# Two and two shift transfers of 128 target rows, and plain fp32 sums for the first two half steps

## The chip, the cores and the metric

The kernel runs on one core of a Trainium2 chip. The metric is the device time of one execution in microseconds. Before the change three runs took 1301.92, 1305.81 and 1307.23 us; their median is 1305.81.

## The reference

```python
def _attn_ref(u, v, z):              # batch 8, S = 2496, D = 256, d_qk = 64
    scores = (1.0 / S) * np.matmul(z, z.transpose(0, 2, 1))
    attn = np.maximum(scores, 0.0) ** 2
    return u * np.matmul(attn, v)

def _moe_ref(x, phi, w1, w2):        # x: 19968 x 256, phi: 256 x 32, 8 experts, 4 slots each
    logits = x @ phi
    d = softmax over the tokens of logits
    slot_input = d.T @ x
    slot_out = relu(slot_input[e] @ w1[e]) @ w2[e]     for every expert e
    c = softmax over the slots of logits
    return c @ slot_out
```

All inputs and outputs are fp32. `x` is the attention output with batch and sequence taken together.

## The kernel before, in words

**Attention.** A batch is cut into five chunks of up to 512 queries, and a chunk into ten *half steps* of 256 keys each (class `Half`, 400 in all). For a half step PE computes the scores of 256 keys against 512 queries, ACT applies relu and square (`r`), the result is split into a high and a low fp16 part (`ph`, `pl`; a cast on ACT or DVE, then a subtraction on DVE), and PE adds three products to the accumulator `acc`: high by v high, high by v low, low by v high (`sums_halves`, `sums_whole`). v is split in the same way by `load_v`'s `high` (ACT) and `low` (DVE), after a scaling by `v_by` that comes from the energy of all ten loads of v (`squares`, `largest`, `scale_v`). The scores are symmetric, so a block above the diagonal is transposed by DVE into `y`, stored to DRAM (`turned`) and fetched later in place of new scores. Scores of half step h+2 are issued between the two phases of the sums of half step h. `finish_chunk` (line 593) multiplies `acc` by `out_by` and by u into `xg`.

**Opening** (lines 964 to 1009). SP issues five loads of z and ten of v. `measure_z` bounds z (DVE), sums the bounds on PE into the PSUM tile `idle`, and makes power-of-two factors. `keep_busy` issues matmuls of ones whose result nothing reads. `prepare_first` (line 411) makes the scores and parts of half steps 0 and 1; ACT measures nine loads of v and DVE one. `scale_v` turns the largest energy around on PE. Then v is split load by load (`split_first_v`) and the loop at line 1010 begins with the sums of half step 0.

**Soft MoE on the side.** For every 1024 finished tokens `groups(q)` (line 633) returns a list of 15 steps, of which the main loop runs one in nearly each half step (line 1017): logits, exponentials, four transposed blocks and one of the exponentials into the SBUF tile `y` (32 partitions by 4 by 576, four times), then the *shifts* (line 627). A shift copies 32 partitions of `y` to one slot of `xt`, so that tokens lie on partitions. Each shift is four transfers of 32 rows. The shifts stand at steps 7, 9, 11 and 13 (line 785), and the last step hands `slot_sums` (line 715) to the next group's `logits`, where PE reads all of `xt` (the trace names these matmuls `lg<-xt`).

**What sets the order.** All engines run in program order. All transfers are issued by SP, one after the other: an SP entry that waits for its source holds up all behind it. Nearly all instructions are recorded under line 74, the wrapper that keeps the order, so they are told apart by the names of their tiles.

Of the kernel before, what the change touches and what calls it, by code (L numbers as in the profile page):

```python
# [77 lines left out]
def attn_soft_moe_kernel(ctx, tc, uT, v, zz, phi, ww, outT):  # L78
# [21 lines left out]


    cw = cpool.tile([P, NG, P], F32, name="cw")
    zt, vt_, zraw = {}, {}, {}

    nudge = cpool.tile([P, 1], F32, name="nudge")
    ones = nc.const_aps.tensor(1.0, [P, 512], BF16)
# [74 lines left out]
    def load_v(b, i):  # L181
        raw = raws.tile([P, 2, D], F32, tag="raw", name=f"vr_{b}_{i}", bufs=NRAW)
        sp.dma_start(raw, v[b, :, 2 * i : 2 * i + 2, :])
        by = v_by[b % 2][:, i : i + 1]
# [52 lines left out]
    def open_loads():  # L237
        for p in range(NP):
            bound, z_splits[p] = load_z(0, p)
            first_z.append(bound)  # L240
        order = [i for p in range(NP) for i in ((2 * p + 1, 2 * p) if p == NQ - 1 else (2 * p, 2 * p + 1))]
        for i in order:
            squares, *two = load_v(0, i)
            first_v.append(squares)
            v_splits.append(two)


    ident = cpool.tile([P, P], F32, name="ident")
# [52 lines left out]
    class Half:  # L301
        def __init__(self, b, ch, p, w, at, part):
            self.b, self.ch, self.p, self.w, self.at = b, ch, p, w, at
            rank = BLOCKS[b == B - 1].index
            mine, keys = rank(ch[0]), rank(p)

            self.turned = keys < mine
            self.turns = keys > mine

            self.opens, self.lends, self.borrows = part == 0, part == 2, part == 3  # L310

            self.padded = ch[0] == NQ - 1
            self.tiles = [4 * p + 2 * w, 4 * p + 2 * w + 1]
            self.begins, self.ends = at == 0, at == 2 * NP - 1

    halves = []
    for b in range(B):
# [90 lines left out]
            ]  # L408
        return [t[:, j] for t in quarters[i]]

    def prepare_first(k):


        r = wa.tile([P, 2, QC], F32, tag="r", name=f"r_{k}", bufs=4)
        pend[k] = hi, lo = high_low(k)
        ps, _ = scores(k)

        def relu():
            act.activation(r, ps, AF.Relu, scale=2.0**-22)

        def square():
            if k:
                act.activation(r, r, AF.Square)
            else:
                dve.tensor_mul(r, r, r)

        def high():
            dve.tensor_copy(hi, r)

        def low():  # L430
            dve.tensor_sub(lo, r, hi)

        return relu, square, high, low

    def prepare(k):

        x = halves[k]
        n = x.ch[2]
# [2 lines left out]
        if x.turned:  # L441
            whole = arriving.pop(k)
            run(middle)
        else:
# [10 lines left out]
        cast = act.copy if x.turned or (x.turns and x.at % 3) else dve.tensor_copy  # L455
        run(turning)
        pieces = [(whole, slice(0, P), cast)]
        if x.borrows:
# [82 lines left out]
    def sums_halves(k, acc, phase, before):  # L541
# [15 lines left out]
        for i in range(len(todo[0])):  # L557
            for h, rows in enumerate(HALF):
                vp, pp = todo[h][i]
                c = h ^ phase ^ side[0]  # L560
                mm = pe.matmul(
                    totals(acc, c, x), vp[rows, c * P : (c + 1) * P], columns(pp[rows], x),
                    start=(x.begins and phase == 0 and i == 0),
                    stop=(x.ends and phase == 1 and i == len(todo[0]) - 1),
                )
                if before is not None:
                    await_(mm, before)
                    before = None
# [6 lines left out]
    def sums_whole(k, acc):  # L575

        x = halves[k]
        hi, lo = pend[k]
        for t, kt in enumerate(x.tiles):
            assert kt < KT - 1  # L580
            vt = vt_[x.b, kt // 2][:, kt % 2]
            for c in range(2):
                for i, (l, r) in enumerate(((0, hi), (1, hi), (0, lo))):
                    pe.matmul(
                        totals(acc, c, x), vt[:, l, c * P : (c + 1) * P], columns(r[:, t], x),
                        start=(x.begins and t == 0 and i == 0),
                        stop=(x.ends and t == 1 and i == 2),
                    )

# [3 lines left out]
    def finish_chunk(b, ch, acc):  # L593
# [3 lines left out]
        while s < n:  # L597
            q, o = divmod(t0 + s, 1024)
            w = min(n - s, 1024 - o)
            if q not in xg_:  # L600
                xg_[q] = wk.tile([P, 2, 1024], F32, tag="xg", name=f"xg_{q}")
            for c in (slice(0, 1), slice(1, 2)) if t0 + n == N else (slice(0, 2),):
                dve.scalar_tensor_tensor(
                    xg_[q][:, c, o : o + w], acc[:, c, s : s + w], out_by[b % 2][:, j : j + 1],
                    ut[:, c, s : s + w], op0=ALU.mult, op1=ALU.mult,
                )
            if o + w == 1024:
                work.extend(groups(q))
            s += w
# [16 lines left out]

    def shift(src, a):


        for b in range(4):  # L630
            sp.dma_start(xt[32 * b : 32 * b + 32, a], src[32 * a : 32 * a + 32, b])

    def groups(q):

# [153 lines left out]

# [167 lines left out]

    idle = acc_ps.tile([P, 2, QC], F32, tag="acc", name="idle")

    def keep_busy(n):
        for _ in range(n):
            for h, rows in enumerate(HALF):
                pe.matmul(idle[:, h], ones[rows, 0:P], ones[rows], start=True, stop=True)
# [10 lines left out]
    def measure_v(n):  # L975
        for _ in range(n):
            first_v.pop(0)()

    def measure_z(js):
        for p in range(*js.indices(NP)):  # L980
# [12 lines left out]
    for f in first[1:]:  # L993
        f()
    second[0]()
    second[1]()
    raise_z(1)
    keep_busy(8)
    first_v.pop()(dve)
    largest(0)  # L1000
    scale_v(0, idle)
    second[2]()
    split_first_v()
    second[3]()
    split_first_v()
    for p in range(2, NP):
        raise_z(p)
    prepare(2)
    acc = None
    for h, x in enumerate(halves):  # L1010
        if x.begins:
# [8 lines left out]
        ahead = [k for k in range(h + 2 + (h > CATCH), h + 3 + (h >= CATCH)) if k < len(halves) and k >= 3]  # L1020
        split_first_v()
        if not ahead and h < 1:
            run(middle)
            run(turning)
            run(behind)
            sums_halves(h, acc, 1, sums_halves(h, acc, 0, None))
        elif ahead and not halves[ahead[0]].turned:
# [318 lines left out]
```

## Time and profile before

| | |
|---|---|
| runs | 1301.92, 1305.81, 1307.23 us, median 1305.81 |
| profiled execution | 1299.81 us, span 1298.0 us |
| PE busy | 1255.5 us, 97% of the span |
| DVE busy | 1100.1 us, 85% |
| ACT busy | 933.3 us, 72% |
| DMA | 297 MB, 74.7% of the 16 DMA engines' span |

The profile shows one execution. PE means TensorE matmuls, PEld its weight loads, DVE VectorE, ACT ScalarE, SP the engine that issues transfers. In a timeline row the columns are start, duration, engine, line, operation, output and inputs, count, and in brackets the idle time just before with what ended it. PEclk is the share of full clock that TensorE was granted: 1.00 is 2.4 GHz, 0.50 is 1.2 GHz. A profiled duration covers an instruction from start to end, and neighbours in one engine's queue overlap by up to 0.1 us.

### The profile page before, as it was taken

Reading aid. Unit: us, or ns where it says so; the run is one execution under the profiler, and the core shown is the slowest. Engines: PE = TensorE matmul, PEld = TensorE weight load, DVE = VectorE, ACT = ScalarE, POOL = GpSimd, SP = SyncE. Lnnn points to the kernel's source line nnn. Section 1 sums busy time; section 2 is a strip of 40 time slices with the busy share of each in tenths; the row PEclk is TensorE's granted clock in tenths of the full one; section 3 lists DMA queues with packets and bytes.
Section 4 is the critical chain, followed back from the end, with each engine's and each line's share of the span. In section 5 each row is a group of like instructions: output and inputs, shape, how many; then the busy total and the mean of one; then the engine's idle time right before and its main releaser. Section 6 shows DMA issues by size and latency. Waiting matters only on the chain.

```text
span 1298.0 us, 27630 instructions
## 1 busy us (share of the span) xinstructions
PE 1255.5 (97%) x10963; PEld 634.2 (49%) x10963; DVE 1100.1 (85%) x1587; ACT 933.3 (72%) x1217; POOL 3.7 (0%) x22
## 2 busy tenths in 40 slices
PE   8999999999999999999999999999999999899984
PEld 3445454545445444545445444454545454345752
DVE  7888898789998899789998799889998799766663
ACT  7878797687857788586958688587976778564553
POOL 0000000000000000000000000000000000000000
PEclk8999999999999999999999999999999999999985
DMA  4868758793888758785788757887587768979769
GB/s 142 239 181 271 226 135 252 242 277 118 202 288 260 241 132 226 256 260 168 186 257 259 252 141 202 266 260 225 145 250 242 265 164 227 288 221 321 290 250 383
DMA packets 136402, 298.88 MB, mean 230 GB/s; under 512 B 17872, under 2 KB 38864, under 8 KB 124240
## 3 DMA queue, kind: packets, MB, share of 16 engines
q1 hardware_dynamic: 136272, 297.11, 74.7%
q8 instruction: 86, 1.41, 0.4%
q14 instruction: 44, 0.36, 0.1%
HBM read 162.04 MB, written 113.77 MB: 212 GB/s over the span
## 4 chain that ended last, share of the span: by engine, by line
PE 72%; DVE 8%; DMA 7%; ACT 5%; SPq 4%; issue 3%; DVEq 0%; ACTq 0%; POOLq 0%
PE acc L74 57%; PE sc L74 9%; SPq L74 4%; DVE y L74 3%; ACT r L74 3%; DVE pl L74 2%; PE lg L74 2%; DMA xt<-y 2%; DMA r<-turned 2%; PE pf L74 2%; ACT ot L74 1%; DMA rd<-lent 1%; ACT ph L74 1%; DVE v L74 1%; DVE ph L74 1%
## 5 line engine op out<-in xcount | busy, mean ns | idle before, releaser
L74 PE MATMUL acc<-ph,v 64*128 64x512 f16 (+5 forms) x5036 | 941.1, 369 | 2.6 <-DVE v L74 1.8
L74 PEld LDWEIGHTS <-v 64*128 64x128 f16 (+1 forms) x7554 | 491.4, 95 | 505.8 <-issue 38.5
L74 PE MATMUL acc<-pl,v 64*128 64x512 f16 (+5 forms) x2518 | 624.6, 368 | 1.7 <-DVE pl L74 1.4
L74 DVE TENSOR_TENSOR pl<-r,ph 128x1024 f16<-128x1024 f32 (+1 forms) x410 | 467.1, 1146 | 110.9 <-ACT ph L74 99.5
L74 ACT CAST ph<-r 128x1024 f16<-128x1024 f32 (+1 forms) x286 | 288.7, 1017 | 124.1 <-DMA r<-turned 55.9
L74 ACT ACTIVATE r<-sc 128x1024 f32<-128x1024 f32 (+1 forms) x242 | 229.0, 946 | 128.7 <-PE sc L74 122.8
L74 ACT ACTIVATE r<-r 128x1024 f32<-128x1024 f32 (+1 forms) x241 | 237.4, 985 | 6.9
L74 DVE STREAM_TRANSPOSE y<-r 128x1024 f32<-128x1024 f32 x160 | 198.0, 1238 | 0.0
L74 PE MATMUL sc<-z,z 64*128 64x512 f16 x912 | 128.1, 376 | 0.4 <-ACT r L74 0.2
L74 PEld LDWEIGHTS <-z 64*128 64x128 f16 x1380 | 75.5, 94 | 70.6 <-issue 2.7
L74 DVE CAST ph<-r 128x1024 f16<-128x1024 f32 (+1 forms) x124 | 74.2, 598 | 12.2 <-ACT r L74 11.6
L74 ACT ACTIVATE v<-vr,v_by 128x512 f16<-128x512 f32 x80 | 57.1, 717 | 9.5 <-DVE v_by L74 8.7
L74 DVE SCALAR_TENSOR_TENSOR xg<-acc,out_by,ut 128x1024 f32<-128x1024 f32 (+7 forms) x57 | 51.5, 926 | 10.0 <-PE acc L74 5.6
L74 DVE SCALAR_TENSOR_TENSOR v<-vr,v_by,v 128x512 f16<-128x512 f32 x80 | 58.5, 732 | 0.1
L74 ACT ACTIVATE vq<-vr 128x512 bf16<-128x512 f32 x79 | 49.2, 622 | 11.4 <-DMA vr<-in_v 11.2
L74 PE MATMUL sc<-z 64*128 64x512 f16 (+1 forms) x468 | 53.0, 321 | 0.0
L74 DVE STREAM_TRANSPOSE y<-xg 128x512 f32<-128x512 f32 x72 | 49.4, 687 | 0.0
L74 DVE COPY ot<-pf 128x1024 f32<-128x1024 f32 (+1 forms) x20 | 24.0, 1198 | 20.8 <-PE pf L74 20.8
L74 ACT COPY ot<-pf 128x1024 f32<-128x1024 f32 (+1 forms) x20 | 19.8, 991 | 24.7 <-PE pf L74 24.7
L74 PE MATMUL lg<-xt 64*32 64x256 f32 x576 | 23.8, 392 | 9.6 <-DMA xt<-y 4.8
L74 ACT CAST ph<-rd 128x512 f16<-128x512 f32 x36 | 21.8, 606 | 12.1 <-DMA rd<-lent 12.1
L74 DVE TENSOR_TENSOR pl<-rd,ph 128x512 f16<-128x512 f32 x36 | 23.9, 664 | 6.2 <-ACT ph L74 6.2
(187 smaller groups left out, 543.7 us busy)
## 6 DMA issues: line engine op xcount, KB each, us to landing
turned<-y SPq DMA_DIRECT2D x320, 256.0 KB, 5.0
r<-turned SPq DMA_DIRECT2D x76, 1024.0 KB, 6.3
xt<-y SPq DMA_DIRECT2D x288, 72.0 KB, 3.6
vr<-in_v SPq DMA_DIRECT2D x80, 256.0 KB, 5.4
outT<-ot SPq DMA_DIRECT2D x18, 1024.0 KB, 6.8
ut<-in_uT SPq DMA_DIRECT2D x31, 512.0 KB, 6.1
lent<-yd SPq DMA_DIRECT2D x144, 64.0 KB, 3.3
rd<-lent SPq DMA_DIRECT2D x36, 256.0 KB, 4.7
```

Of the source, the lines that this page charges most:

```text
L74: return lambda *a, **k: self.tc.keep_in_program_order(f(*a, **k))
```

## The change

**Shifts.** A shift becomes one transfer of 128 target rows: target row 4k+b takes block b of source partition k (before, target row 32b+k). All columns of a row move together, and PE sums over the rows, so the order of rows does not matter. Two shifts are issued at step 7 and two at step 9; steps 11 and 13 do nothing. The last two groups have no shifts in either kernel.

**Opening.** Half steps 0 and 1 no longer wait for the scaled and split v. Their relu and square stay fp32 (`r0`, `r1`), and `plain_sums` multiplies them with the raw fp32 v, in eight fp32 matmuls of 128 by 128 by 512 into a PSUM accumulator `plain`. In half step 4 ACT copies `plain`, scaled by `ratio`, into `xg`, and `finish_chunk` of the first chunk adds `acc` to it before its final product. DVE measures five loads of v and ACT five. The scores of half step 1 go to the accumulator's bank, those of half step 2 are prepared before the loop, and v loads 0 and 1 are split last. `idle` moves to another bank.

```diff
     def shift(src, a):
-        for b in range(4):
-            sp.dma_start(xt[32 * b : 32 * b + 32, a], src[32 * a : 32 * a + 32, b])
+        sp.dma_start(xt[:, a], src[32 * a : 32 * a + 32])
...
-        shifts = [lambda a=a: shift(y(), a) for a in range(4)]
+        shifts = [lambda a=a: (shift(y(), a), shift(y(), a + 1)) for a in (0, 2)]
...
-            todo = [logits, ex, *blocks, e, shifts[0], c0, shifts[1], c1, shifts[2], c2, shifts[3]]
+            todo = [logits, ex, *blocks, e, shifts[0], c0, shifts[1], c1, rest, c2, rest]
...
+    def plain_sums(k, r, acc, t):
+        for c in range(2):
+            pe.matmul(
+                acc[:, c], vraw[k][:, t, c * P : (c + 1) * P], r[:, t],
+                start=(k == 0 and t == 0), stop=(k == 1 and t == 1),
+            )
...
+                sums = acc[:, c, s : s + w]
+                if t0 == 0:
+                    sums = xg_[q][:, c, o : o + w]
+                    dve.tensor_add(sums, sums, acc[:, c, s : s + w])
...
-    keep_busy(6)
+    keep_busy(8)
...
     raise_z(0)
-    keep_busy(1)
-    first = prepare_first(0)
-    first[0]()
-    second = prepare_first(1)
-    measure_v(2 * NP - 1)
+    keep_busy(3)
+    acc = next_acc()
+    r0, relu = first_scores(0, scale=2.0**-30)
+    relu()
+    act.activation(r0, r0, AF.Square)
+    r1, relu = first_scores(1, acc, scale=2.0**-30)
+    relu()
+    keep_busy(4)
     measure_z(slice(1, NP))
...
     raise_z(1)
-    keep_busy(8)
+    dve.tensor_mul(r1, r1, r1)
+    plain_sums(0, r0, plain, 0)
+    r2, relu = first_scores(2)
+    plain_sums(0, r0, plain, 1)
+    measure_v(4, act)
+    measure_v(4, dve)
+    relu()
+    measure_v(1, act)
     first_v.pop()(dve)
     largest(0)
+    plain_sums(1, r1, plain, 0)
     scale_v(0, idle)
+    plain_sums(1, r1, plain, 1)
+    prepare(2, r2)
...
+    landing[4] = [lambda: act.activation(xg_[0][:, :, 0:QC], plain, AF.Identity, scale=ratio)]
+    halves[2].starts = True
+    prepare(3)
...
+        if h < 2:
+            continue
```

**SP's queue in the second batch**, from the first shift of a group to its last. `xt<-y` are the shifts, `r<-turned` and `rd<-lent` fetches, `vr` and `ut` loads of v and u, `turned<-y` stores. Before:

```order
L74 DMA xt<-y_3190 32x576 x4
L74 DMA vr_7_3407<-in_v 128x512
L74 DMA vr_8_3429<-in_v 128x512
L74 DMA ut_3447<-in_uT 128x2x512
L74 DMA vr_9_3449<-in_v 128x512
L74 DMA xt<-y_3190 32x576 x4
L74 DMA rd_3492<-lent_3_3356 128x512
L74 DMA r_3494<-turned_0_4_2496 128x2048
L74 DMA xt<-y_3190 32x576 x4
L74 DMA r_3586<-turned_1_4_2772 128x2048
L74 DMA turned_3_4_3636<-y_3524 32x4x512 x4
L74 DMA xt<-y_3190 32x576 x4
```

With the change:

```order
L74 DMA xt<-y_3119 128x1x576 x2
L74 DMA vr_7_3334<-in_v 128x512
L74 DMA vr_8_3356<-in_v 128x512
L74 DMA ut_3374<-in_uT 128x2x512
L74 DMA vr_9_3376<-in_v 128x512
L74 DMA xt<-y_3119 128x1x576 x2
L74 DMA rd_3417<-lent_3_3285 128x512
L74 DMA r_3419<-turned_0_4_2429 128x2048
L74 DMA r_3507<-turned_1_4_2701 128x2048
L74 DMA turned_3_4_3557<-y_3449 32x4x512 x4
```

The second half of the set now goes out ahead of two fetches and a store that it used to follow, and the set is 4 entries instead of 16.

**PE's queue in the opening**, around the matmul that serves `scale_v` (`idle<-ident,few`). Before:

```order
L74 MATMUL idle_117<-const-bfloat16-1.0 128x512
L74 MATMUL idle_117<-ident_94,few0_92 128x128
L74 MATMUL sc_2_288<-cw_78 128x512 x2
L74 LDWEIGHTS v_0_0_123
L74 MATMUL acc_0_298<-ph_0_202,v_0_0_123 128x512
```

With the change (`plain` is the new accumulator, `vr` raw v):

```order
L74 MATMUL idle_117<-tops0_80,const-float32-1.0 128x4 x2
L74 MATMUL plain_118<-r_0_211,vr_0_0_140 128x512 x2
L74 MATMUL sc_2_247<-cw_78 128x512 x2
L74 MATMUL plain_118<-r_0_211,vr_0_0_140 128x512 x2
L74 MATMUL plain_118<-r_1_217,vr_0_1_142 128x512 x2
L74 MATMUL idle_117<-ident_94,few0_92 128x128
L74 MATMUL plain_118<-r_1_217,vr_0_1_142 128x512 x2
L74 MATMUL sc_3_302<-cw_78 128x512 x2
L74 LDWEIGHTS v_0_2_126
L74 MATMUL acc_0_210<-ph_2_287,v_0_2_126 128x512
```

Plain sums stand where fillers stood, and the first split sums are those of half step 2, behind the scores of half step 3.

**DVE's queue at the end of the first chunk**, from the difference of half step 9 to that of half step 12 (the number behind `pl_` and `ph_` is the half step). Before:

```order
L74 TENSOR_TENSOR pl_9_615<-r_9_608,ph_9_614 128x1024
L74 STREAM_TRANSPOSE y_8_558<-r_9_608 128x2x16x32
L74 CAST ph_10_648<-r_10_642 128x1024
L74 TENSOR_TENSOR pl_10_649<-r_10_642,ph_10_648 128x1024
L74 TENSOR_TENSOR z_0_1_120<-cw_78,z_0_1_120 128x512
L74 CAST ph_11_689<-r_11_683 128x1024
L74 TENSOR_TENSOR pl_11_690<-r_11_683,ph_11_689 128x1024
L74 SCALAR_TENSOR_TENSOR xg_0_705<-acc_0_298,out_by0_90,ut_0_364 128x2x512
L74 TENSOR_TENSOR pl_12_709<-r_12_487,ph_12_708 128x1024
```

With the change:

```order
L74 TENSOR_TENSOR pl_9_564<-r_9_557,ph_9_563 128x1024
L74 SCALAR_TENSOR_TENSOR v_0_0_124<-vr_0_0_140,v_by0_88,v_0_0_124 128x2x256
L74 STREAM_TRANSPOSE y_8_507<-r_9_557 128x2x16x32
L74 CAST ph_10_599<-r_10_593 128x1024
L74 TENSOR_TENSOR pl_10_600<-r_10_593,ph_10_599 128x1024
L74 TENSOR_TENSOR z_0_1_121<-cw_78,z_0_1_121 128x512
L74 SCALAR_TENSOR_TENSOR v_0_1_125<-vr_0_1_142,v_by0_88,v_0_1_125 128x2x256
L74 CAST ph_11_642<-r_11_636 128x1024
L74 TENSOR_TENSOR pl_11_643<-r_11_636,ph_11_642 128x1024
L74 TENSOR_TENSOR xg_0_300<-xg_0_300,acc_0_210 128x2x512
L74 SCALAR_TENSOR_TENSOR xg_0_300<-xg_0_300,out_by0_90,ut_0_312 128x2x512
L74 TENSOR_TENSOR pl_12_662<-r_12_436,ph_12_661 128x1024
```

Two low parts of v and one addition have come in between.

## Rows read from the trace of the kernel before

**Rows 1.** Page, part 1: busy time, share of the span, instructions.
```profile
PE 1255.5 (97%) x10963; PEld 634.2 (49%) x10963; DVE 1100.1 (85%) x1587; ACT 933.3 (72%) x1217; POOL 3.7 (0%) x22
```
**Rows 2.** Windows, PE alone: stretch, length, PE busy, granted clock, DMA share, GB/s.
```profile
25.02:1195.00 1169.98, 1156.08 (x9851) 1.00 0.75 224
```
**Rows 3.** Waits of PE, whole span: total, times, longest.
```profile
PE lg L74 <- DMA xt<-y: 4.8, 7, 1.2
PE lg L74 <- DMA w_raw<-in_w: 4.8, 1, 4.8
...
PE acc L74 <- DVE pl L74: 1.4, 3, 0.7
```
**Rows 4.** Timeline of PE at the last but one set of slot sums.
```profile
1131.55 1.09 PE L74 MATMUL lg<-xg,phi_sb 64*32 64x256 f32 x32
1137.42 2.30 PE L74 MATMUL lg<-xt 64*32 64x256 f32 x32 [4.77 <-DMA w_raw<-in_w]
1139.65 0.94 PE L74 MATMUL acc<-ph,v 64*128 64x512 f16 x4
```
**Rows 5.** Timeline of SP in the same place.
```profile
1132.04 2.41 SPq L74 DMA_DIRECT2D xt<-y  x4
1134.49 1.06 SPq L74 DMA_DIRECT2D w_raw<-in_w  x2
```
**Rows 6.** Windows, PE alone, behind that wait (columns as in rows 2).
```profile
1138.00:1139.00 1.00, 1.00 (x25) 0.50 0.74 166
```
**Rows 7.** Timeline of PE at the last set of slot sums.
```profile
1194.80 1.45 PE L74 MATMUL lg<-xt 64*32 64x256 f32 x32 [0.16 <-DMA xt<-y]
```
**Rows 8.** Page, part 6: issues, KB each, median us from issue to landing.
```profile
turned<-y SPq DMA_DIRECT2D x320, 256.0 KB, 5.0
...
xt<-y SPq DMA_DIRECT2D x288, 72.0 KB, 3.6
```
**Rows 9.** Tile xt: SP's issues, ns shortest, median, longest.
```profile
L74 SPq DMA_DIRECT2D xt<-y x288: 507/589/2367, 118.6 to 1190.3; - x144
```
**Rows 10.** Waits of ACT, whole span.
```profile
ACT ph L74 <- DMA r<-turned: 55.9, 19, 6.6
```
**Rows 11.** Timeline of DVE in the opening.
```profile
11.09 0.17 DVE L74 TENSOR_SCALAR norm<-idle 128x4 int32<-128x4 int32 x1 [2.25 <-PE idle L74]
...
15.09 0.69 DVE L74 CUSTOM_DVE_ANT_0 vq<-vr 128x512 bf16<-128x512 f32 x1
...
28.10 1.23 DVE L74 TENSOR_TENSOR pl<-r,ph 128x1024 f16<-128x1024 f32 x1
```
**Rows 12.** Groups of DVE by form, 20 to 60 us: busy, mean ns.
```profile
L74 DVE STREAM_TRANSPOSE y<-r 128x1024 f32<-128x1024 f32 x8 | 9.9, 1239 | 0.0
L74 DVE SCALAR_TENSOR_TENSOR v<-vr,v_by,v 128x512 f16<-128x512 f32 x9 | 6.7, 742 | 0.0
...
L74 DVE TENSOR_SCALAR cw<-cw,z_by 128x512 f32<-128x512 f32 x3 | 1.3, 482 | 0.0
```
**Rows 13.** Timeline of DVE at the end of the first chunk.
```profile
49.67 1.23 DVE L74 TENSOR_TENSOR pl<-r,ph 128x1024 f16<-128x1024 f32 x1
...
55.03 0.70 DVE L74 CAST ph<-r 128x1024 f16<-128x1024 f32 x1 [0.47 <-ACT r L74]
...
58.16 1.22 DVE L74 TENSOR_TENSOR pl<-r,ph 128x1024 f16<-128x1024 f32 x1
```
**Rows 14.** Timeline of PE: scores of half steps 3 and 14.
```profile
24.16 1.02 PE L74 MATMUL sc<-cw 64*128 64x512 f32 x4
25.02 0.59 PE L74 MATMUL acc<-ph,v 64*128 64x512 f16 x4
...
60.67 0.81 PE L74 MATMUL sc<-z,z 64*128 64x512 f16 x6
```
**Rows 15.** Windows in the opening: PE, PEld, DVE, ACT, POOL busy, then clock, DMA share, GB/s.
```profile
5.00:10.00 5.00, 3.19 (x10) 1.23 (x10) 3.62 (x12) 2.68 (x6) 0.00 (x0) 0.71 1.04 378
10.00:15.00 5.00, 4.25 (x22) 1.97 (x19) 3.78 (x7) 4.81 (x15) 0.00 (x0) 0.60 0.97 348
```

More of the change, by code (lines that the diff above doesn't have):

```diff
@@ L102, in attn_soft_moe_kernel @@
     cw = cpool.tile([P, NG, P], F32, name="cw")
-    zt, vt_, zraw = {}, {}, {}
+    zt, vt_, zraw, vraw = {}, {}, {}, {}
     nudge = cpool.tile([P, 1], F32, name="nudge")
@@ L183, in load_v @@
         sp.dma_start(raw, v[b, :, 2 * i : 2 * i + 2, :])
+        vraw[i] = raw
         by = v_by[b % 2][:, i : i + 1]
@@ L245, in open_loads @@
             v_splits.append(two)
+        v_splits.extend(v_splits[:2])
+        del v_splits[:2]
     ident = cpool.tile([P, P], F32, name="ident")
@@ L314, in __init__ @@
             self.begins, self.ends = at == 0, at == 2 * NP - 1
+            self.starts = self.begins
     halves = []
@@ L409, in high_low, with first_scores, prepare @@
         return [t[:, j] for t in quarters[i]]
-    def prepare_first(k):
+    def first_scores(k, ps=None, scale=2.0**-22):
         r = wa.tile([P, 2, QC], F32, tag="r", name=f"r_{k}", bufs=4)
[L415 to L435, printed above, removed]
+        ps, _ = scores(k, ps)
+        return r, lambda: act.activation(r, ps, AF.Relu, scale=scale)
+    def plain_sums(k, r, acc, t):
[4 more added lines that the diff above has]
+            )
+    def prepare(k, r=None):
         x = halves[k]
@@ L443, in prepare @@
             run(middle)
+        elif r is not None:
+            run(middle)
+            act.activation(r, r, AF.Square)
+            whole = r.rearrange("p h (a r) -> p h a r", r=P)
         else:
@@ L454, in prepare @@
         hc, lc = (t[:, :, :m].rearrange("p h (a r) -> p h a r", r=P) for t in (hi, lo))
-        cast = act.copy if x.turned or (x.turns and x.at % 3) else dve.tensor_copy
+        cast = act.copy if x.turned or (x.turns and x.at % 3 and k > 2) else dve.tensor_copy
         run(turning)
@@ L562, in sums_halves @@
                     totals(acc, c, x), vp[rows, c * P : (c + 1) * P], columns(pp[rows], x),
-                    start=(x.begins and phase == 0 and i == 0),
+                    start=(x.starts and phase == 0 and i == 0),
                     stop=(x.ends and phase == 1 and i == len(todo[0]) - 1),
@@ L585, in sums_whole @@
                         totals(acc, c, x), vt[:, l, c * P : (c + 1) * P], columns(r[:, t], x),
-                        start=(x.begins and t == 0 and i == 0),
+                        start=(x.starts and t == 0 and i == 0),
                         stop=(x.ends and t == 1 and i == 2),
@@ L602, in finish_chunk @@
             for c in (slice(0, 1), slice(1, 2)) if t0 + n == N else (slice(0, 2),):
+                sums = acc[:, c, s : s + w]
+                if t0 == 0:
+                    sums = xg_[q][:, c, o : o + w]
+                    dve.tensor_add(sums, sums, acc[:, c, s : s + w])
                 dve.scalar_tensor_tensor(
-                    xg_[q][:, c, o : o + w], acc[:, c, s : s + w], out_by[b % 2][:, j : j + 1],
+                    xg_[q][:, c, o : o + w], sums, out_by[b % 2][:, j : j + 1],
                     ut[:, c, s : s + w], op0=ALU.mult, op1=ALU.mult,
@@ L955, in between_last @@
             copy_x(act.copy, ps, xt_last[k - 1])
-    idle = acc_ps.tile([P, 2, QC], F32, tag="acc", name="idle")
+    idle = ms_ps.tile([P, 2, 512], F32, tag="ms", name="idle")
+    plain = acc_ps.tile([P, 2, QC], F32, tag="acc", name="plain")
     def keep_busy(n):
@@ L963, in keep_busy @@
             for h, rows in enumerate(HALF):
-                pe.matmul(idle[:, h], ones[rows, 0:P], ones[rows], start=True, stop=True)
+                pe.matmul(plain[:, h], ones[rows, 0:P], ones[rows], start=True, stop=True)
     dve.memset(nudge, 2.0**-40)
@@ L970, in attn_soft_moe_kernel, with measure_v @@
     constants()
-    keep_busy(6)
+    keep_busy(8)
     def raise_z(p):
         dve.tensor_scalar_mul(zraw[0, p], zraw[0, p], z_by[0][:, p : p + 1])
-    def measure_v(n):
+    def measure_v(n, engine):
         for _ in range(n):
-            first_v.pop(0)()
+            first_v.pop(0)(engine)
     def measure_z(js):
@@ L986, in attn_soft_moe_kernel @@
     raise_z(0)
-    keep_busy(1)
-    first = prepare_first(0)
-    first[0]()
-    second = prepare_first(1)
-    measure_v(2 * NP - 1)
+    keep_busy(3)
[6 more added lines that the diff above has]
+    keep_busy(4)
     measure_z(slice(1, NP))
[L993 to L996, printed above, removed]
     raise_z(1)
-    keep_busy(8)
+    dve.tensor_mul(r1, r1, r1)
[6 more added lines that the diff above has]
+    measure_v(1, act)
     first_v.pop()(dve)
     largest(0)
+    plain_sums(1, r1, plain, 0)
     scale_v(0, idle)
-    second[2]()
+    plain_sums(1, r1, plain, 1)
+    prepare(2, r2)
     split_first_v()
-    second[3]()
     split_first_v()
@@ L1007, in attn_soft_moe_kernel @@
         raise_z(p)
-    prepare(2)
-    acc = None
+    ratio = few[0][:, 3:4]
+    dve.tensor_scalar_mul(ratio, v_by[0][:, 0:1], 2.0**16)
+    xg_[0] = wk.tile([P, 2, 1024], F32, tag="xg", name="xg_0")
+    landing[4] = [lambda: act.activation(xg_[0][:, :, 0:QC], plain, AF.Identity, scale=ratio)]
+    halves[2].starts = True
+    prepare(3)
     for h, x in enumerate(halves):
-        if x.begins:
+        if x.begins and h:
             chunk = h // (2 * NP)
@@ L1019, in attn_soft_moe_kernel @@
         behind.extend(landing.pop(h, ()))
-        ahead = [k for k in range(h + 2 + (h > CATCH), h + 3 + (h >= CATCH)) if k < len(halves) and k >= 3]
+        ahead = [k for k in range(h + 2 + (h > CATCH), h + 3 + (h >= CATCH)) if k < len(halves)]
         split_first_v()
[L1022 to L1027, printed above, removed]
+        if ahead and not halves[ahead[0]].turned:
             turn = sums_halves(h, acc, 0, None)
```

## The prediction, made before the changed kernel ran

> **What bounds the kernel now.** I read the page's busy shares first. PE is busy 97% of the span and DVE 85% [rows 1], so a stage is faster only where PE waits. The windows of PE place its idle time: between 25 us, where the opening is over, and 1195 us, PE is busy 1156.1 of 1170.0 us at the full clock [rows 2]. These 13.9 us are nearly all that can be won there. The list of PE's waits says whom it waits for [rows 3]: 4.8 us in seven pieces for the landing of `xt`, and 4.8 us in one piece that carries the name of a weight load. The timeline shows that this piece stands before the same matmuls, `lg<-xt` [rows 4]. They read nothing but `xt`. SP issued the last shift of that set from 1132.04 to 1134.45 and began two weight loads at 1134.49 [rows 5]; PE could go on at 1137.42, three microseconds after the last shift, which is about the usual time to landing of 3.6 us [rows 8]. So I take it as a wait for the shift, and the label for the transfer next to it. The two waits make 9.6 of the 13.9 us.
>
> **The shifts, step by step.** Per set, 16 transfers of 72 KB become 4 of 288 KB. The fourth shift stood at step 13, the slot sums follow after step 14: one half step of cover, about 3 us, against 3.6 us to landing and whatever SP had queued ahead. Now the second pair stands at step 9, so five half steps lie between, about 15 us.
>
> What a transfer of 288 KB takes is not in the trace. The nearest row is the store of `y`, 256 KB out of the same 32 partitions, at 5.0 us to landing; from below it is bounded by the 72 KB transfer's 3.6 us, from above by four of them in turn, 14.4 us [rows 8]. I take 5.2 us, near the store. Both ends are under 15 us, so the waits go: **9.6 us**.
>
> The long wait also cost clock. PE stood for 4.77 us, and from 1137 to 1140 us the clock was at 0.50, the 1.2 GHz level [rows 6]. The 32 matmuls that took 1.45 us at the other set [rows 7] took 2.23 us there, from 1137.42 to 1139.65 [rows 4], and the next twelve sums started at the same level. I count 0.8 for the first and 0.3 for the second, together **1.1 us**.
>
> SP issues 216 entries fewer at 0.59 us each [rows 9], 127 us of SP's time. I cost that at nothing: behind PE's other waits stand DVE results (1.4 us for `pl` [rows 3]), and these would cover it. Work moved past other queues: the second pair, 576 KB, now goes out ahead of two fetches and a store. At the 0.38 MB/us of a full DMA queue (378 GB/s [rows 15]) that delays them by 1.5 us at most, and takes the same from what follows. ACT has been late for fetches 19 times, 55.9 us in all [rows 10], and passed nearly none of it to PE, so I cost it at nothing too; the third rival prices it otherwise. DVE's and PE's work on the sets is unchanged.
>
> **The opening, step by step.** PE first. A pair of fp32 score matmuls of 512 columns occupies it from 24.16 to 25.02, 0.86 us, at the full clock [rows 14]; two of them at a time fill the 128 rows that one plain matmul fills, so I price the eight plain matmuls at 0.86 us each, 6.9 us. They replace 48 split matmuls and lie where PE had fillers. With v measured as late as before, PE could begin the scores of half step 5 some 2.9 us sooner than before. That gain doesn't last, because DVE becomes the bound:
>
> - DVE gets the bounds' sum at about 10.4 us (before, it waited 2.25 us for it until 11.09 [rows 11]). It then scales a z block (0.5 [rows 12]), squares `r1` (1.2, as a difference of that shape [rows 11]) and measures five loads of v at about 0.75. With the factors that is done at 16.9 us; before, the last measure ran from 15.09 to 15.8 [rows 11]. So the scale of v comes about 1 us **later**, at 19.
> - Then a cast and a difference (0.7 and 1.2), two low parts of v (0.7 each), three z blocks (1.3), one transposition (1.2) and a cast [rows 11 to 13]. The difference of half step 3 starts at 26.0; before, at 28.10 [rows 11]. DVE is 2.1 us ahead.
> - From there to the difference of half step 9 the queues are alike: 49.67 [rows 13] becomes about 47.6.
> - Then the change adds two low parts of v (0.66 each from start to start, 0.74 long [rows 12]) and an addition as large as a difference (1.2), 2.5 us, and takes out the 0.47 us that DVE waited at 55.03 [rows 13]. The difference of half step 12 starts at 58.16 - 2.1 + 2.5 - 0.5 = 58.1; before, at 58.16 [rows 13].
> - PE comes to half step 12 about 1 us earlier and waits at its third product until 59.3. The rest of the phase takes 0.9 us, so the scores of half step 14 start at 60.2 instead of 60.67 [rows 14]. After that DVE has room, and PE keeps what it has: **0.4 us**.
>
> ACT's copy of `plain` (1 us) lies in half step 4 beside PE's sums. Had it no cover it would cost 1 us.
>
> All this needs the full clock. Before, the granted clock was 0.71 from 5 to 10 us and 0.60 from 10 to 15 us, with PE busy 3.2 and 4.3 of 5 us [rows 15]. The change gives PE four more filler pairs ahead of the first scores and six behind, so I take the full level from the start. At 1.2 GHz throughout, the eight plain matmuls, three pairs of scores and the fillers would take twice as long, 11 us more, of which DVE's own chain covers 2 to 3: the opening would lose 8.5. These are the ends for the opening, a gain of 2.9 and a loss of 8.5. The Trainium skill, in "TensorE: Matmul & The Clock Gate", Part 1, says that the throttled level is the default and that sustained activity lifts it; by that rule alone the plain sums could start at the low level and the sum would be near the lossy end. The trace agrees that both levels occur in this opening, and that denser work was followed by the higher one.
>
> **The sum.** 9.6 + 1.1 + 0.4 = 11.1 us, rounded down to 11 for waits that may come in their place. Against the profiled execution's 1299.8 us that is 1288.8; the median of the runs shown is 6.0 us higher, 1305.8, which gives **1295 us**.
>
> **The rivals.**
>
> *The next wait steps in.* Where PE stood for `xt`, the casts and differences of the next half step may be ready hardly sooner, because ACT waits for its fetches there. For it: 55.9 us of ACT's waits for fetches [rows 10]. Against it: PE waited only 1.4 us for `pl` in the whole span [rows 3], and differences run two half steps ahead. If half of the 10.7 us is lost again, the gain is 5.5 us and the time 1300.
>
> *The opening runs at the low clock.* Loss 8.5, gain 10.7: the time is about 1304. The skill's rule above is this rival. Against it stand the extra fillers.
>
> *Slower: the 128-row transfer lands late.* Four rows lie behind each other in one source partition, and a transfer still touches only 32 source partitions. If the big transfer moved no faster than four small ones in turn and the two of a pair came one after the other as well, the second would land far behind the 15 us of cover. It decides from a landing of 15 us on; at 16.5 us PE waits 1.5 us in each of 18 sets, 27 us, in place of the 10.7: 1322. Against it: the store out of the same partitions lands in 5.0 us [rows 8].
>
> *The change doesn't do what it says:* a set that still ends late, because SP reaches the entry late. SP's wait for `y` is the same for both pairs, and two steps of other entries are skipped, so I fold this into the first rival.
>
> **How the numbers follow.** Forecast (a gain of 7 to 14 us) 0.66; next wait 0.20; low clock 0.08; late landing 0.06. About 0.5%, 6.5 us, is what a measurement of this kernel can tell from no change. The first rival reaches over it in a fifth of its cases, so faster gets 0.66 + 0.04 = 0.70, same 0.16 + 0.08 = 0.24, slower 0.06. The range goes up to 1303, which takes in the first rival and most of the second; down to 1287, which is 2.5 us more in the opening and 5 us for a median that lies lower among its runs, as the profiled execution did.
>
> **What would show it.** Right: no wait of `lg<-xt` over 0.2 us, 72 issues of `xt` landing near 5 us, PE idle 4 to 5 us between 25 us and the last set, and the scores of half step 14 at 60 to 61 us. Wrong: waits of `lg<-xt` that remain; waits of `acc` for `pl` or `ph` that grow by several microseconds; a granted clock of 0.5 between 7 and 14 us; a start of the scores of half step 14 that moves by over 2 us.

## The result and the profile after

The changed kernel took 1284.58 us (median of four runs, 1281.32 to 1286.19), the kernel before in the same comparison 1304.51 us (four runs, 1301.92 to 1307.23): ratio 0.9844, 95% interval 0.9814 to 0.9874. It is faster by some 20 us, where 11 were forecast, and lies below the range (1287 to 1303). The two profiled executions stand 15.9 us apart, 1299.81 and 1283.93 us, their spans 16.0 us, 1298.0 and 1282.0. The span is what the next lines can account for.

The page's busy shares of the changed kernel (against [rows 1]) and PE's window (against [rows 2]):

```profile
PE 1247.7 (97%) x10931; PEld 634.3 (49%) x10931; DVE 1099.7 (86%) x1594; ACT 929.1 (72%) x1209; POOL 4.2 (0%) x22
```
```profile
25.02:1195.00 1169.98, 1162.50 (x10016) 1.00 0.76 230
```

PE's share is 97% as before: of the 16.0 us of span, 7.8 are busy time and 8.2 idle time, so it is not waits alone that went. Between 25 and 1195 us PE is idle for 7.5 us instead of 13.9. PE's waits, against [rows 3] (columns: total, times, longest):

```profile
PE acc L74 <- DVE pl L74: 3.2, 5, 0.7
PE acc L74 <- DVE ph L74: 2.6, 1, 2.6
PE acc L74 <- DVE v L74: 2.3, 7, 0.7
```

No wait of `lg<-xt` is left, neither for `xt` nor under the name of a weight load. In its place stand one wait of 2.6 us for `ph`, small ones for `pl` before 80 us, and those for `v` at the start of each batch, which were there before. (The largest entry of both lists is left out here and in [rows 3]: `pf` waits for ACT's copies behind the last set, 10.6 us before and 12.7 after.)

**Where the 16 us came from** is read by the start of each set of slot sums in both timelines. First one of the five late sets in the middle of the kernel before, then a set of the changed kernel:

```profile
1013.37 1.09 PE L74 MATMUL lg<-xg,phi_sb 64*32 64x256 f32 x32
1015.41 1.56 PE L74 MATMUL lg<-xt 64*32 64x256 f32 x32 [0.95 <-DMA xt<-y]
1016.91 0.61 PE L74 MATMUL acc<-ph,v 128*128 128x512 f16 x2
```
```profile
1123.07 1.09 PE L74 MATMUL lg<-xg,phi_sb 64*32 64x256 f32 x32
1123.95 1.07 PE L74 MATMUL lg<-xt 64*32 64x256 f32 x32
1124.95 0.61 PE L74 MATMUL acc<-ph,v 64*128 64x512 f16 x4
```

From the start of the logits to the first sums behind the set, the late one takes 3.54 us and the undisturbed one 1.88. The named wait is 0.95, but the set is 1.66 us longer: the slot sums start 1.16 us late, and then take half as long again (1.50 us to the next start, not 1.00). Why they run slower is not shown: the granted clock reads 1.00 there. So the lead of the changed kernel grows at each such set. It is (start of a set before, less the start after):

| between | lead gained, us |
|---|---|
| start and the first set (90.79 to 87.73) | 3.06 |
| first set and 415 us, small waits | 0.71 |
| five late sets, 415 to 1014 us | 8.20 |
| 1071 to 1131 us of the kernel before | -3.49 |
| the long set at 1131.55 (8.10 us from start to sums, [rows 4]) and the sums behind it | 6.55 |
| the last set (2.64 to 1.89 us) | 0.75 |
| end | 0.2 |

The sets gave 15.5 us, the opening 3.1, and one place took 3.5 back. That place is in these lines of SP, ACT and PE:

```profile
1099.98 0.33 SPq L74 DMA_DIRECT2D r<-turned  x1
1100.36 0.42 SPq L74 DMA_DIRECT2D w_own<-in_w  x1
1100.84 1.20 SPq L74 DMA_DIRECT2D xt<-y  x2
1102.08 0.59 SPq L74 DMA_DIRECT2D rd<-lent  x1
1102.72 4.96 SPq L74 DMA_DIRECT2D turned<-y  x4
...
1110.81 0.62 ACT L74 CAST ph<-rd 128x512 f16<-128x512 f32 x1 [5.82 <-DMA rd<-lent]
...
1109.56 0.38 PE L74 MATMUL acc<-pl,v 128*128 128x512 f16 x1
1112.54 0.61 PE L74 MATMUL acc<-ph,v 64*128 64x512 f16 x4 [2.60 <-DVE ph L74]
```

The fetch of `rd` is issued behind a fetch of 1 MB, a weight load of 512 KB and two shifts of 288 KB; it lands 8.7 us after its issue, ACT's cast waits 5.82 us for it, and PE 2.60 us. The windows there (columns as in [rows 15]) show full DMA engines, and a lower clock behind PE's wait:

```profile
1100.00:1105.00 5.00, 5.00 (x50) 2.22 (x45) 4.75 (x5) 4.89 (x6) 0.00 (x0) 1.00 1.04 388
1105.00:1111.00 6.00, 4.94 (x23) 2.06 (x21) 1.24 (x2) 0.19 (x1) 0.00 (x0) 1.00 1.02 359
1111.00:1116.00 5.00, 3.34 (x18) 1.39 (x20) 4.41 (x9) 2.32 (x3) 0.00 (x0) 0.71 0.93 321
```

The transfers, against [rows 8]: 72 shifts of 288 KB land in 5.6 us, beside 3.6 us for a quarter of that.

```profile
xt<-y SPq DMA_DIRECT2D x72, 288.0 KB, 5.6
```

**The opening**, PE and then DVE, against [rows 11, 13, 14]:

```profile
5.96 1.13 PE L74 MATMUL sc<-cw 64*128 64x512 f32 x4 [0.47 <-DVE cw L74]
6.93 1.02 PE L74 MATMUL acc<-cw 64*128 64x512 f32 x4
...
9.30 1.99 PE L74 MATMUL plain<-r,vr 128*128 128x512 f32 x4
...
56.74 0.39 PE L74 MATMUL acc<-pl,v 64*128 64x512 f16 x2 [0.73 <-DVE pl L74]
57.60 0.83 PE L74 MATMUL sc<-z,z 64*128 64x512 f16 x6
```
```profile
9.41 0.17 DVE L74 TENSOR_SCALAR norm<-idle 128x4 int32<-128x4 int32 x1 [0.70 <-PE idle L74]
...
23.78 1.23 DVE L74 TENSOR_TENSOR pl<-r,ph 128x1024 f16<-128x1024 f32 x1
...
44.95 1.23 DVE L74 TENSOR_TENSOR pl<-r,ph 128x1024 f16<-128x1024 f32 x1
...
53.02 1.21 DVE L74 TENSOR_TENSOR xg<-xg,acc 128x1024 f32<-128x1024 f32 x1
54.26 1.28 DVE L74 SCALAR_TENSOR_TENSOR xg<-xg,out_by,ut 128x1024 f32<-128x1024 f32 x1
55.47 1.22 DVE L74 TENSOR_TENSOR pl<-r,ph 128x1024 f16<-128x1024 f32 x1
```

The bounds' sum comes at 9.41 (forecast 10.4), the difference of half step 3 at 23.78 (26.0), that of half step 12 at 55.47 (58.1), the scores of half step 14 at 57.60 (60.2). DVE does bound: PE waits 0.73 us there. DVE's lead over the kernel before is 4.3 us at half step 3, 4.7 at half step 9 (44.95 against 49.67 [rows 13]) and 2.7 at half step 12. So the added work took 2.0 us of it, as forecast, but from a lead larger than forecast (2.1).

### The profile page after: what moved, and what is told of

Same layout as the page of the kernel before. It is cut to its first block, busy times and chain, and to the rows that moved or that the text cites. A ratio compares the mean times of both kernels' runs of the same rounds, so it can differ in the third digit from the quotient of the medians.

```text
span 1282.0 us, 27265 instructions
## 1 busy us (share of the span) xinstructions
PE 1247.7 (97%) x10931; PEld 634.3 (49%) x10931; DVE 1099.7 (86%) x1594; ACT 929.1 (72%) x1209; POOL 4.2 (0%) x22
## 4 chain that ended last, share of the span: by engine, by line
PE 82%; DVE 8%; ACT 3%; DMA 3%; issue 2%; SPq 1%; DVEq 0%; ACTq 0%
PE acc L74 67%; PE sc L74 9%; DVE y L74 3%; PE lg L74 2%; DVE pl L74 2%; DMA outT<-ot 1%; ACT r L74 1%; PE pf L74 1%; DVE v L74 1%; ACT ot L74 1%; DVE ph L74 1%; DMA rd<-lent 1%; ACT ph L74 1%; SPq L74 1%; PE h L74 1%
## 5 line engine op out<-in xcount | busy, mean ns | idle before, releaser
L74 PE MATMUL acc<-ph,v 64*128 64x512 f16 (+4 forms) x5004 | 936.6, 369 | 4.9 <-DVE ph L74 2.6
L74 DVE CAST ph<-r 128x1024 f16<-128x1024 f32 (+1 forms) x123 | 73.3, 596 | 10.6 <-ACT r L74 10.1
L74 ACT ACTIVATE vq<-vr 128x512 bf16<-128x512 f32 x75 | 46.6, 621 | 3.6 <-DMA vr<-in_v 3.5
L74 DVE SCALAR_TENSOR_TENSOR z<-zr,z_by,z 128x512 f16<-128x512 f32 x35 | 25.6, 732 | 0.0
```

Of the source, the lines that this page charges most:

```text
L74: return lambda *a, **k: self.tc.keep_in_program_order(f(*a, **k))
```

## The experiments

Each ratio is to the kernel before on the same chip, with its 95% interval.

**The two halves, and the two parts of the shifts.** *The shifts alone*, with the old opening:

> The shifts' part alone on the kernel before: one transfer of 128 rows each, two at step 7 and two at step 9, the opening as before. Theory (the late landings of xt cost what the sets of slot sums took from start to end above an undisturbed set, 15.2 us over seven sets, and a new wait of 3.5 us for a lent block takes part of it back): 11 to 13 us faster than before, every set of slot sums 1.9 us long, one wait of PE for ph near 1112 us. Rival (the opening carries more than the 3.1 us that it shows by 88 us): less than 9 us faster.

Measured: 1287.86 us, ratio 0.9879 (0.9863 to 0.9895). By the medians that is 15.9 us, more than the 11 to 13 expected; the two profiled executions stand 11.6 us apart (1299.81 and 1288.24). All sets take 1.89 us but one of 2.38 that the kernel before has too. PE's new wait for `ph`, 1.8 us, is there too: it belongs to the shifts.

*The opening alone*, with the old shifts:

> The opening alone, shifts as before. Theory: 3 us faster than before, reached by the scores of half step 14 (57.6 us against 60.67) and kept; the late sets of slot sums stay, 3.4 to 8.1 us long. Rival (the forecast's sum, DVE eats the gain): 0.4 us. Rival (the earlier start also moves transfers so that late sets change): more than 6 us either way.

Measured: 1300.55 us, ratio 0.9981 (0.9967 to 0.9995). The first set starts at 87.91, 2.9 us ahead of the profiled kernel before, but the last one only 0.74 us ahead. Most of the lead goes behind the long set: it is 2.35 us at that set's start, and behind it the clock is 0.50 from 1135 to 1141 us (before, from 1137 to 1140). The medians keep 3.2 us. The sets are late as before:

```profile
PE lg L74 <- DMA w_raw<-in_w: 4.9, 1, 4.9
PE lg L74 <- DMA xt<-y: 4.1, 7, 1.0
```

The two halves, 15.9 and 3.2 us of medians, make up 19.1 of the 20 us of the whole.

*Moved, not merged*: sixteen transfers of 32 rows, eight at step 7 and eight at step 9.

```diff
-        shifts = [lambda a=a: shift(y(), a) for a in range(4)]
+        shifts = [lambda a=a: (shift(y(), a), shift(y(), a + 1)) for a in (0, 2)]
...
-            todo = [logits, ex, *blocks, e, shifts[0], c0, shifts[1], c1, shifts[2], c2, shifts[3]]
+            todo = [logits, ex, *blocks, e, shifts[0], c0, shifts[1], c1, rest, c2, rest]
```

> The kernel before with its transfers of 32 rows, but two shifts (eight transfers) at step 7 and two at step 9. It tells place from size. Theory (the place in the queue is what made xt late): all sets 1.9 us long, 9 to 14 us faster than before. Rival (SP's time for 16 entries makes it late): sets still up to 1 us longer in places, and less than half of the gain of e1.

Measured: 1314.67 us, ratio 1.0091 (1.0073 to 1.0109), **slower than before** and outside both expectations. The waits for `xt` are gone, but others came:

```profile
PE sc L74 <- ACT r L74: 12.2, 17, 1.9
...
PE acc L74 <- DVE ph L74: 9.7, 4, 6.5
```

SP's lines at the place of the longest one show why:

```profile
1126.36 8.66 SPq L74 DMA_DIRECT2D xt<-y  x8
1135.12 0.53 SPq L74 DMA_DIRECT2D rd<-lent  x1
```

Eight entries in a block hold up the fetch of `rd` by 8.66 us, where two of 288 KB hold it up by 1.20 (above). The Trainium skill, "DMA: Bandwidth & Descriptors", Rules for kernel authors, advises to coalesce many small transfers into one; at 72 KB against 288 KB this run agrees. The bytes are the same 576 KB here and there: what the merging saves is SP's time.

*Merged, not moved*: one transfer of 128 rows each at steps 7, 9, 11 and 13.

```diff
-        for b in range(4):
-            sp.dma_start(xt[32 * b : 32 * b + 32, a], src[32 * a : 32 * a + 32, b])
+        sp.dma_start(xt[:, a], src[32 * a : 32 * a + 32])
```

> The kernel before with one transfer of 128 rows per shift, left at steps 7, 9, 11 and 13. Theory (place): the last transfer is issued in 0.6 us instead of 2.4 to 5.7 but takes 5.6 us to land instead of 3.6, so sets stay late in places: 2 to 7 us faster. Rival (SP's time): the late sets are gone and the gain is that of e1.

Measured: 1296.53 us, ratio 0.9942 (0.9924 to 0.9960), 7.2 us faster by the medians, just above the 2 to 7 expected for the place. The set at 1131 us still takes 6.56 us, five others 2.5 to 3.6; `lg<-xt` waits 7.9 us in five pieces for `xt`, and 0.8 in one that carries the name of a load of v. Neither part gives the 15.9 us: the place takes the wait away, and the merging pays for the place.

**What holds the opening and the end.** *The change with the old fillers*:

```diff
-    keep_busy(8)
+    keep_busy(6)
...
-    keep_busy(3)
+    keep_busy(1)
...
-    keep_busy(4)
```

> The changed kernel with the filler matmuls of before: keep_busy 6, 1 and none in place of 8, 3 and 4. Theory (the full clock in the opening is held by the added fillers, and is what the opening's 3 us rest on): the granted clock shows 0.5 somewhere between 6 and 20 us, the first pieces run at half speed, and the first set of slot sums' logits starts at 89 to 92 us where the change has 87.7; the time is 1286 to 1289. Rival (the plain sums themselves, because they wait for nothing that v's measure gives, and DVE is the bound): fewer fillers change nothing, the first set stays at 87 to 88.3 us, the time within 1283 to 1286.

Measured: 1285.09 us, ratio 0.9848 (0.9829 to 0.9868); the first set at 91.11, 3.38 us later than with the fillers. PE ran its first pairs of scores and the first plain sums at half speed:

```profile
6.48 2.08 PE L74 MATMUL sc<-cw 64*128 64x512 f32 x4 [0.70 <-DVE cw L74]
8.35 1.92 PE L74 MATMUL acc<-cw 64*128 64x512 f32 x4
...
10.83 3.78 PE L74 MATMUL plain<-r,vr 128*128 128x512 f32 x4
```

Of the 3.38 us only 1.21 are left at the last set, since PE, coming later, waits less and stays at full clock near 1115 us. The first set lies where the theory put it, the time, 1285.09 us, where the rival did. Nor are the 3.38 us the price of the fillers alone, since two profiles of kernels with all of them ran that pair slowly too (below).

*The second pair of shifts at step 11*:

```diff
-            todo = [logits, ex, *blocks, e, shifts[0], c0, shifts[1], c1, rest, c2, rest]
+            todo = [logits, ex, *blocks, e, shifts[0], c0, rest, c1, shifts[1], c2, rest]
```

> The changed kernel with the second pair of shifts at step 11 in place of step 9, so that in the last but one group it is issued behind the fetch of rd. Theory (the 2.6 us that PE waits for ph at 1112.5 come from that fetch, queued behind 576 KB of shifts): the wait falls to under 0.7 us, the late sets of slot sums still run in 1.9 to 2.1 us since three half steps of cover, 9 us, are above a landing of 5.6 us, and the last set starts 2 to 3.5 us earlier than the change's 1178.5: about 1281. Rival 1 (the wait at 1112.5 is of ACT's own making): it stays, and the time is that of the change, 1284.6 within 1.5. Rival 2 (the 4.8 us wait of before comes back, since SP reaches step 11 late): a wait of 1 us or more at lg<-xt in the last sets, 1286 to 1290.

Measured: 1283.87 us, ratio 0.9853 (0.9831 to 0.9875), within the uncertainty of the change and not the 1281 expected. The wait for `ph` fell to 1.0 us, but two sets in the middle are late again, in place of the last ones that the second rival named. In the first of them SP began to issue the second pair 7.7 us before the slot sums were due at 530.6 us, less than the 9 us that I had counted, and PE could go on 9.3 us after it:

```profile
529.72 1.09 PE L74 MATMUL lg<-xg,phi_sb 64*32 64x256 f32 x32
532.18 1.10 PE L74 MATMUL lg<-xt 64*32 64x256 f32 x32 [1.37 <-DMA vr<-in_v]
```
```profile
522.89 4.05 SPq L74 DMA_DIRECT2D xt<-y  x2
```

*All four shifts at step 7*:

```diff
-        shifts = [lambda a=a: (shift(y(), a), shift(y(), a + 1)) for a in (0, 2)]
+        shifts = [lambda: [shift(y(), a) for a in range(4)], lambda: None]
```

> The changed kernel with all four shifts at step 7, 1152 KB in one block. Theory (a block of shifts delays the fetches queued behind it by its bytes): PE's waits for ph and pl behind the shifts grow in several groups, and the time is 1285 to 1291, 0.5 to 6 us over the change. Rival (fetches at step 7 have more lead than at step 9, and only the last but one group's rd fetch is tight): the wait at 1112.5 goes, and the time is 1281 to 1283.

Measured: 1298.45 us, ratio 0.9955 (0.9941 to 0.9969), 14 us over the change and far above both expectations. PE's waits for `ph` grew from 2.6 to 9.2 us in four pieces:

```profile
PE acc L74 <- DVE ph L74: 9.2, 4, 4.2
```

*The old opening with more fillers*, beside the new shifts:

```diff
-    keep_busy(6)
+    keep_busy(8)
...
-    keep_busy(1)
+    keep_busy(3)
...
     second = prepare_first(1)
+    keep_busy(4)
```

> The shifts of the change, with the opening of before, to which only fillers are added: keep_busy 8 and 3 where it had 6 and 1, and 4 more behind the scores of half step 1. Theory (the opening's gain is one of clock): the clock is at 1.0 from 5 to 15 us, the first set of slot sums starts at 88 to 89.5 us instead of the 90.8 to 94 of the old opening, and the time is 1284.5 to 1286.5. Rival (the plain sums are what gains): the clock rises but PE waits for the split v, the first set starts at 90 to 92 us and the time is 1287 to 1289, like that with the shifts alone (1287.9).

Measured: 1288.92 us, ratio 0.9887 (0.9868 to 0.9905), that of the shifts alone. The second pair of scores ran at full speed (1.13 us), the first did not (1.94). DVE got the bounds' sum at 12.27 us, hardly earlier than in the three profiles of that opening with both pairs slow (12.44 to 12.51), since the added fillers stand ahead of it, and the first set starts at 92.49:

```profile
12.27 0.17 DVE L74 TENSOR_SCALAR norm<-idle 128x4 int32<-128x4 int32 x1 [3.00 <-PE idle L74]
```

In this place fillers alone gain nothing, and the plain sums are needed. What the old opening would do with a full clock from 5 us on, as the theory wanted it, is not shown.

**The new wait.** *Seven weight loads early*, in the changed kernel:

```diff
-        58: [0], 56: [1], 54: [2], 51: [3], 49: [4], 47: [5], 45: [6], 43: [7], ...
+        66: [0, 1], 65: [2, 3], 64: [4, 5], 63: [6], 43: [7], ...
```

(their tiles are taken at 66 too)

> The changed kernel with the seven loads of w_own, 512 KB each, moved from 58 to 45 half steps before the end to 66 to 63 before it: behind the fetch of rd at 1036 us, into the stretch from 1040 to 1055 us where the DMA engines are busy 0.19 to 0.45 of the time. Theory (from 1070 to 1120 us the DMA engines are full, 0.95 to 1.03, and the wait for ph at 1112.5 and the clock that it costs are the bytes, not the place of the shifts in the queue): 3.6 MB less in that stretch, so rd lands in time, the wait falls under 0.5 us, the last set starts 3 to 4 us earlier than the change's 1178.5, and the time is 1280 to 1282. Rival (the queue order: rd behind two shifts of 288 KB): the wait stays over 1.5 us and the time within 1 us of the change.

*The same with few fillers*:

> The kernel with the early w_own loads and the fillers of before (6, 1 and none). Theory (the fillers keep the clock and are worth 3.4 us at the first set, which the full DMA engines near 1100 us ate in the run with few fillers alone): with room on the DMA engines the loss stays to the end, so this kernel is 2.5 to 3.5 us slower than the one with early loads and all fillers: 1283 to 1285, and its last set starts that much later. Rival (the few fillers cost nothing in most executions, the profiled one was unlucky): within 1 us of it.

*The second pair at step 11 in one group alone*:

```diff
+            if q == NQG - 4:
+                todo[9], todo[11] = rest, shifts[1]
```

> The changed kernel with the second pair of shifts at step 11 instead of 9 in one group alone, the one whose shifts go out at 1088 and 1101 us, so that the fetch of rd is issued ahead of this pair. Theory (full DMA engines: the fetch of 1 MB and the stores that are already under way decide, and with the pair at step 11 everywhere rd still took 8.8 us to land): the wait at 1112.5 is still 1 to 2.6 us, the time within 1.5 us of the change, 1283.5 to 1286. Rival (queue order): the wait falls under 0.6 us and the time to about 1281.

*The change again*, on the same chip:

> The changed kernel itself, beside the three others on one chip. Both theories: 1283.5 to 1286; in the profile the first set of slot sums' logits starts at 87.5 to 88.5 us as in the four profiles with all fillers so far, and PE waits 2 to 3 us for ph near 1112 us. If the first set starts over 2 us later, the clock of the opening varies with the new fillers too.

Measured: early loads 1282.23 us (0.9809 to 0.9844), with few fillers 1284.33 (0.9826 to 0.9865), step 11 in one group 1281.56 (0.9805 to 0.9840), the change 1285.94 (0.9831 to 0.9871). In the change, PE comes 2.1 us later than in its first profile and waits 2.44 us for `ph`. When `rd` was issued and when ACT could use it, in the change and then with the one pair at step 11, both 1.9 to 2.1 us behind the first profile:

```profile
1104.85 0.59 SPq L74 DMA_DIRECT2D rd<-lent  x1
...
1112.78 0.62 ACT L74 CAST ph<-rd 128x512 f16<-128x512 f32 x1 [5.66 <-DMA rd<-lent]
```
```profile
1102.38 0.98 SPq L74 DMA_DIRECT2D rd<-lent  x1
...
1110.66 0.62 ACT L74 CAST ph<-rd 128x512 f16<-128x512 f32 x1 [3.79 <-DMA rd<-lent]
```

Ahead of the pair the fetch comes 2.1 us earlier, PE's wait falls from 2.44 to 0.57 us, and the lead over the change grows by 3.6 us, with the clock at 1.00 from 1111 to 1118 us, where the change has 0.86. My theory, that only the bytes count, was wrong here: the place in the queue counts. With the early loads the DMA share from 1100 to 1111 us is 0.89, and in the change's first profile it was 1.04 and 1.02 there. The wait falls to 1.03 us, not under the expected 0.5, so moving other transfers away helps too:

```profile
1040.00:1055.00 15.00, 14.80 (x147) 7.42 (x147) 14.24 (x21) 13.36 (x17) 0.00 (x0) 1.00 0.75 294
...
1100.00:1111.00 11.00, 10.05 (x72) 4.33 (x68) 7.11 (x8) 6.66 (x9) 0.00 (x0) 1.00 0.89 280
```

With few fillers the first set starts 1.2 us later (89.01 against 87.83) and the last 2.1; the medians stand 2.1 us apart, short of the expected 2.5 to 3.5, though 1284.33 lies in the expected 1283 to 1285.

**Both edits together**:

> The early w_own loads and the second pair of shifts at step 11 in the one group, together. Theory (the DMA engines are full there, and what stands ahead of the fetch of rd counts by its bytes, wherever it comes from; each edit alone made rd land 1.6 and 2.0 us earlier against PE's own progress): rd is in time, PE's wait for ph near 1110 us is under 0.3 us, the clock stays at 1.0 there, the last set starts 0.5 to 1 us earlier against the first set than with either edit, and the time is 1279.5 to 1281.5. Rival (the two edits save the same wait, and another transfer is then late, the next fetch or the second pair itself): a wait of over 0.5 us stays near 1110 us or lg<-xt waits near 1120 us, and the time is 1281.5 to 1283.

Measured: **1280.37 us**, ratio 0.9825 (0.9809 to 0.9841), the lowest median of all, though with step 11 in one group alone the ratio is the same within the uncertainty. From the first set to the last it takes 1086.7 us, 0.45 less than that one and 0.92 less than the early loads, near the expected 0.5 to 1. PE has no wait for `ph` left, `lg<-xt` does not wait, and PE is busy throughout at the full clock:

```profile
1100.00:1111.00 11.00, 11.00 (x84) 1.00 0.91 271
1111.00:1118.00 7.00, 7.00 (x49) 1.00 0.92 289
```

Both edits act on the same wait, by letting SP come to the fetch sooner. Counted from the first set, SP issues `rd` at 1014.4 and 1015.0 us in the two profiles of the change, at 1013.5 with the early loads, 1012.8 with step 11 in one group and 1012.0 with both. From its issue to its landing the fetch takes about as long in all five, 7.9 to 8.7 us. Whether it is SP's time for the entries ahead or their bytes on full DMA engines is not told apart, since both edits take away both.

## Why the prediction was wrong, point by point

The step that failed is the price of the waits for `xt`: the mechanism was right, but 10.7 us stood in the sum for what measured 15.5. Two smaller terms were off as well, 0.4 us for the opening, which gave 3.1, and nothing for a next wait, which took 3.5.

- **"The waits go: 9.6 us", and "1.1 us" of clock.** The mechanism was right: no `xt` wait is left, and the long piece under the weight load's name was a wait for the shift, as I took it. The size was wrong: 15.5 us, not 10.7. I summed the idle time named in the list. Six short sets came to 8.95 us from start to start, where the list has 4.8 in seven pieces; the long one and the sums behind it to 6.55, where I had 4.8 and 1.1. A wait's idle time starts from the modelled end of the matmuls ahead, which lies 0.2 us behind the start of what follows them undisturbed (1123.07 + 1.09 against 1123.95; on PE neighbours overlap by more than the 0.1 us that I named), and slow matmuls behind it are not in it. For the clock I compared with the last set's 1.45 us [rows 7], which was itself disturbed; an undisturbed set of slot sums takes 1.07.
- **A shift of 288 KB lands in "5.2 us".** It took 5.6. The rival of the late landing is out; but with the second pair two steps later two sets were late again, and the longest landing in that run was 9.7 us, so the margin was smaller than the median lets one think.
- **"127 us of SP's time ... at nothing".** Wrong as a cost of nothing. With the old entries in the new place the kernel is 11 us slower than before. Merging alone moved 7 us of medians; SP's time is what lets the shifts stand ahead of the fetches.
- **The first rival, a next wait.** It came, in one place and not spread over the sets: 3.5 us near 1112 us. I had named its cause (the second pair goes out ahead of two fetches, 1.5 us of delay each), and put it at nothing because ACT's lateness elsewhere had hardly reached PE, by sums over the whole span. (The text there says that the third rival prices it; it is the first.) At this place, with the DMA engines full, ACT's lateness of 5.82 us did reach PE.
- **"PE keeps what it has: 0.4 us" in the opening.** It was 3.1 us by the profiles. DVE got the bounds' sum a microsecond earlier than I reckoned, behind fillers that took 1.04 us at 7.79. I also summed full durations of neighbours in DVE's queue, which overlap: the scale of v was done at 17.4 us, 0.6 before the kernel before, where I had 19 and a microsecond behind it. The difference of half step 3 came 2.2 us earlier than forecast, that of half step 12 2.6. DVE's added work did come, in the place forecast.
- **The second rival, the low clock.** It happened in part. Of the eight profiles with the new opening and all fillers, six ran the first pair of scores in 1.13 us and had their first set at 87.7 to 88.1 us; two ran it in 2.08 and had it at 89.6 and 89.9. The loss is 2 us, not 8.5, and not in every execution. That the profile of the change is one of the six is in part luck.
- **The anchor.** I took 11 us from a median. The profiled execution of before was an early one in its opening: it ran the first pair of scores in 1.13 us and its first set starts at 90.79, while the three other profiles with that opening ran it in 2.08 and have the first set at 91.95 to 93.96. So the spans show 3.1 us of gain in the opening where most executions have rather 4, which is a part of the difference between 16 us by profile and 20 by medians. The rest of it stays open.

## What to carry to other kernels

Price a wait by the time from the work ahead of it to the work behind it, against an undisturbed instance of the same piece, and not by the idle time that the list names: here that was 15.5 us against 9.6 named. A transfer that is moved early must be followed through the queue to the fetches that it now precedes, and priced where the DMA engines are full, not by averages. Moving and merging belonged together: merging alone gave 7 us of the 16, moving alone lost 11.

## What the runs showed of the hardware that was not expected

- The clock of the opening differs between executions of the same instructions: the first pair of scores took 1.13 us in some and 2.08 in others, 1.8 times as long, near the ratio of the two levels. In the change's second profile PE had a filler running right up to that pair, and still:

```profile
6.50 2.08 PE L74 MATMUL sc<-cw 64*128 64x512 f32 x4
8.37 1.92 PE L74 MATMUL acc<-cw 64*128 64x512 f32 x4
```

  The Trainium skill, "TensorE: Matmul & The Clock Gate", Part 1, says that how many matmuls run at the low level at the start varies from run to run; these runs agree. With the added fillers ahead of it the first pair ran at the full level in six of nine profiles, in either opening, and with the old ones in one of six. So they do not ensure it; that they make it more frequent is likely, but so few profiles do not show it, nor give a price.
- The column of the granted clock does not show this: in that profile it reads 1.00 over the same stretch.

```profile
5.00:10.00 5.00, 5.00 (x16) 1.00 1.00 368
```

- A late engine wins part of its delay back here. In the profile with few fillers the 3.4 us at the first set were 1.2 at the last, and the opening's 2.9 us of lead, without the new shifts, were 0.7 at the last set.
